# One more filler matmul at the end of each pair, at the head of the wide wo loop and in its steps

## The chip, the cores and the metric

The kernel runs on one core of one Trainium2 chip. The metric is the device time in microseconds (us). A time is the median of several runs, and differences of well under one per cent matter here only as far as they stand clear of the spread of the runs. TensorE is written PE, VectorE DVE, ScalarE ACT, SyncE (which issues the loads) SP.

## The reference

A gated mix of two branches for one token of width 512. Branch A is decode attention over 32 heads with a cache of 16384 positions; branch B is a small gated MLP. Cut to what matters:

```python
g = sigmoid((x * gate_w).sum(-1, keepdims=True))
q = (x @ wq)                       # 32 heads of 128
scores = q @ k_cache.T * 128**-0.5 # k_cache: (1, 32, 16384, 128) bf16
p = softmax(scores)
o = p @ v_cache                    # v_cache: the same shape
a = o.reshape(1, 1, 4096) @ wo     # wo: (4096, 512)
b = gmlp(x, w_in, w_sp, b_sp, w_out)
return g * a + (1 - g) * b
```

The two caches are 134 MB each. Every byte is used once.

## The kernel before

The heads are taken two at a time: 16 pairs. A pair has 8.39 MB of keys and 8.39 MB of values, loaded into three buffers in turn. DVE multiplies the keys by the query, PE sums the products with identity matmuls, ACT makes the exponentials, and PE multiplies them with the values. A load into a buffer is issued by SP when the buffer's last user has signalled.

`fill` is the helper the change uses. It issues 512-column matmuls into a scratch bank whose contents nobody reads. They do no work; they keep PE busy in gaps, so that its clock is not throttled. They load no weights of their own and write partitions 96 and up, so they sit in the last of the four column groups of the array. `warm` does the same over the full width, with weights.

```python
def warm(e, n):
    for j in range(n):
        args = (m_ps[0], ident[:, :], zero[:, :])
        ...  # the first loads the weights, the others repeat with the same ones

def fill(e, m, n=1):
    for _ in range(n):
        matmul_again(nc, e, m_ps[0][96:96 + m, :], ident[:, 0:m], zero[:, :], start=True,
                     stop=True, skip_group_check=True)
```

The end of a pair: a loop of value matmuls, then two fillers, then the wait for ACT's drain of the bank, then four small fp32 matmuls whose end releases the value buffer.

```python
def values(e, p, pa, va):
    ...
    with e.Fori(0, NT) as t:               # 8 steps
        ...                                # 8 value matmuls into d_ps
        ins.then_inc(pv_s, 1)              # ACT drains d_ps after the eighth
        fill(e, 8)
        ...
    o2 = o_ps[:, bass.ds(value(e, p, NP - 1) * 2, 2)]
    fill(e, 8, 2)
    take(e, drn_s)                         # waits for ACT
    for r in range(4):
        ins = e.matmul(o2, lhsT=d_sb[:, r * Dh:(r + 1) * Dh],
                       rhs=pick[:, r * 2:(r + 1) * 2], ...)
    ins.then_inc(pe.sem, 1)                # the value buffer is free
```

After the last pair comes the product with `wo`: four "wide" steps of four matmuls, one in each column group, then 32 narrow matmuls in the first two column groups, in order of the pieces in which `wo` is loaded.

```python
def pe_wide(e):
    ...
    warm(e, 3)
    with e.Fori(0, WIDE // WG) as t:       # 4 steps
        ...                                # 4 matmuls, one in each column group
        ins.then_inc(pe.sem, 1)
        fill(e, 1)
        ...
```

The one choice at the end of a pair is made here:

```python
with nc.body("pe_values", valid_engines=kind):
    values(e, p, pa, va)
    e.reg_alu(p, p, 1, ALU.add)
    e.br_lt(i, NP, on_true="pe_scores", on_false="pe_more")
```

The softmax here doesn't subtract the row's maximum and nothing guards it: scores larger than these inputs give would overflow.

## Time and profile before

| | before |
|---|---|
| median of 3 runs | 651.58 us (651.5 to 651.92) |
| loaded | 279.60 MB, 430 GB/s over the span |
| busy: PE, DVE, ACT | 65%, 52%, 7% |
| one pair's loads at 430 GB/s | 16.78 MB, 39.0 us |

The page of the kernel before: its span, the line of PE's busy time with its share of the span, the busy tenths of the loading engines in 40 equal slices, and what they moved.

```profile
span 650.2 us, 7779 instructions
...
PE 423.5 (65%) x2474; PEld 47.0 (7%) x1312; DVE 335.2 (52%) x156; ACT 46.1 (7%) x114; POOL 2.6 (0%) x11
...
DMA  9999989999999999999999999999999999999898
...
DMA packets 6203, 279.60 MB, mean 430 GB/s; under 512 B 695, under 2 KB 826, under 8 KB 1210
```

Every slice of the DMA row is at 8 or 9 tenths, while no computing engine is above two thirds. 279.60 MB divided by 650.2 us is the 430 GB/s: the whole span is loading.

The view of the line that issues the cache loads, kernel before; the times run from issue to landing.

```profile
DMA to landing us min/median/max: 24.6/34.7/55.0
```

A whole key or value load of 8.39 MB needs 19.5 us at 430 GB/s. Even the quickest load took 24.6 us, so an estimated 5 us (24.6 less 19.5) of older loads stood ahead of it.

The timeline of the kernel before at the end of a pair. Columns: start, duration, engine, line, operation, what it wrote and read, count, and in brackets the idle time before it and what ended that.

```profile
555.13 0.81 PE L91 MATMUL ps_all<-zero,ident 128*8 128x512 bf16 x3
...
556.13 0.59 ACT L606 CAST ps_all<-zero 128x512 f32<-128x512 bf16 x1
...
557.02 1.05 PE L531 MATMUL ps_all<-pick,d_sb 128*128 128x2 f32 x8 [1.08 <-PEq L86]
558.10 0.80 SPq L647 DMA_DIRECT2D bufs<-in_A_k_cache_dram  x2
```

The three fillers at 555.13 are the last one of the value loop and the two of the pair end. PE then sits idle for 1.08 us until ACT has drained and cleared the bank, and the matmuls with `pick` start at 557.02. SP issues the next key load as soon as they are done.

The tail of the kernel before, the same view.

```profile
638.46 0.60 PE L106 MATMUL ps_all<-bufs,p_t 128*8 x8
...
643.38 0.39 PE L106 MATMUL ps_all<-bufs,o 128*1 x4 [0.32 <-PEq L86]
...
645.69 0.39 PE L106 MATMUL ps_all<-bufs,o 128*1 x4 [0.19 <-PEq L86]
...
645.97 1.04 PE L724 MATMUL ps_all<-bufs,o 128*1 128x256 bf16 x16
...
647.28 0.42 PEld L724 LDWEIGHTS ps_all<-bufs,o 128*1 128x1 bf16 x10 [0.36 <-DMA bufs<-in_A_wo_dram]
...
647.96 0.09 PEld L724 LDWEIGHTS ps_all<-bufs,o 128*1 128x1 bf16 x4 [0.26 <-DMA bufs<-in_A_wo_dram]
648.23 0.08 PEld L724 LDWEIGHTS ps_all<-bufs,o 128*1 128x1 bf16 x2 [0.19 <-DMA bufs<-in_A_wo_dram]
...
648.58 0.41 DVE L739 CAST res<-ps_all 1x256 bf16<-1x256 f32 x1 [6.04 <-PE ps_all L724]
```

The last step of value matmuls starts at 638.46 and the final cast of the result at 648.58. The weight loads (PEld) at 647.28, 647.96 and 648.23 are each shown waiting for a piece of `wo`.

### The profile page before, as it was taken

How to read it: one execution, taken by the hardware profiler on the slowest of the kernel's cores; microseconds unless marked ns; L12 is line 12 of the kernel's file. 1: busy time of each engine (PE TensorE's matmuls, PEld its weight loads, DVE VectorE, ACT ScalarE, POOL GpSimd, SP SyncE). 2: the span in 40 equal slices, each digit the busy share in tenths (PEclk: the TensorE clock that was granted, in tenths of full speed). 3: DMA queues.
4: the chain of work that ended last, by engine and by line, in shares of the span. 5: the costliest groups of instructions: out<-in, count | busy, mean ns of one | idle time of the engine just before them, and what ended most of it. 6: DMA issues, size and time to landing. Idle time of an engine off the chain costs nothing. (4 is left out here: it accounts for less than half of the span.)

```text
span 650.2 us, 7779 instructions
## 1 busy us (share of the span) xinstructions
PE 423.5 (65%) x2474; PEld 47.0 (7%) x1312; DVE 335.2 (52%) x156; ACT 46.1 (7%) x114; POOL 2.6 (0%) x11
## 2 busy tenths in 40 slices
PE   0646687847477574857757486584748857478678
PEld 0000000000101000010000101000010100001022
DVE  3457839256280835618165370835628174465600
ACT  2220000100001000010100001000000100001011
POOL 1000000000000000000000000000000000000000
PEclk9959798958889796888969679796977969698979
DMA  9999989999999999999999999999999999999898
GB/s 384 463 419 452 452 387 452 452 444 395 452 452 395 444 452 444 395 452 452 407 431 452 444 395 452 452 427 411 452 452 391 448 452 439 399 431 472 390 431 342
DMA packets 6203, 279.60 MB, mean 430 GB/s; under 512 B 695, under 2 KB 826, under 8 KB 1210
## 3 DMA queue, kind: packets, MB, share of 16 engines
q1 hardware_dynamic: 6194, 279.58, 99.6%
q8 instruction: 1, 0.02, 0.0%
q10 hardware_dynamic: 8, 0.00, 0.0%
HBM read 279.58 MB, written 0.00 MB: 430 GB/s over the span
## 5 line engine op out<-in xcount | busy, mean ns | idle before, releaser
L579 DVE TENSOR_TENSOR bufs<-bufs,qb x64 | 281.4, 4418 | 171.8 <-DVEq L86 171.8
L91 PE MATMUL ps_all<-bufs,ident 128*128 x960 | 257.7, 422 | 0.0
L496 PE MATMUL ps_all<-bufs,ident 128*128 x64 | 28.8, 450 | 154.7 <-PEq L86 154.5
L106 PE MATMUL ps_all<-bufs,p_t 128*8 x1024 | 82.3, 395 | 30.3 <-PEq L86 20.3
L564 DVE TENSOR_REDUCE s_sb<-ps_all 128x64 f32<-128x512 f32 x64 | 44.0, 688 | 92.1 <-DVEq L86 92.1
L91 PE MATMUL ps_all<-zero,ident 128*8 128x512 bf16 (+2 forms) x167 | 59.4, 388 | 0.0
L592 ACT ACTIVATE p_t<-s_sb 64x256 f32 x32 | 13.3, 414 | 462.5 <-ACTq L86 462.1
L496 PEld LDWEIGHTS ps_all<-bufs,ident 128*128 128x128 bf16 x64 | 6.3, 99 | 365.3 <-issue 365.3
L106 PEld LDWEIGHTS ps_all<-bufs,p_t 128*8 x1024 | 19.3, 83 | 163.3 <-issue 161.9
L531 PE MATMUL ps_all<-pick,d_sb 128*128 128x2 f32 x128 | 17.3, 257 | 16.5 <-PEq L86 16.5
L531 PEld LDWEIGHTS ps_all<-pick,d_sb 128*128 128x128 f32 x128 | 16.0, 195 | 34.8 <-issue 34.8
L601 ACT COPY d_sb<-ps_all 128x512 f32<-128x512 f32 x16 | 9.4, 586 | 105.3 <-ACTq L86 105.3
L606 ACT CAST ps_all<-zero 128x512 f32<-128x512 bf16 x15 | 8.8, 589 | 1.7
L675 DVE RECIPROCAL rl<-ps_all 128x32 f32<-128x32 f32 x1 | 0.4, 358 | 12.3 <-PE ps_all L552 12.3
L381 DVE TENSOR_TENSOR bufs<-ps_all,ident 128x896 f32<-128x896 f32 x2 | 2.1, 1086 | 8.7 <-PE ps_all L91 8.7
L676 DVE SCALAR_TENSOR_TENSOR o_sb<-ps_all,g_sb,rl 128x32 bf16<-128x32 f32 x1 | 0.3, 251 | 11.7 <-PE ps_all L531 11.7
L592 ACT ACTIVATION_READ_ACCUMULATOR p_t<-s_sb x32 | 5.9, 185 | 0.0
L321 PE MATMUL ps_all<-xgw,const-float32-1.0 1*128 1x3 f32 x2 | 0.6, 359 | 8.0 <-DVE xgw L317 8.0
L91 PE MATMUL ps_all<-bufs,xb 128*128 x12 | 5.0, 547 | 0.0
L106 PE MATMUL ps_all<-bufs,u 128*1 x14 | 2.6, 372 | 3.1 <-ACT ps_all L427 2.4
L345 PE MATMUL ps_all<-bufs,xb 128*128 x4 | 2.3, 574 | 3.3 <-DMA bufs<-in_B_w_in_dram 3.3
L301 DVE MEMSET ps_all<- 128x3584 f32 x1 | 3.0, 3045 | 1.9 <-PEq L770 1.9
(76 smaller groups left out, 40.9 us busy)
## 6 DMA issues: line engine op xcount, KB each, us to landing
bufs<-in_A_k_cache_dram SPq DMA_DIRECT2D x2, 4096.0 KB, 36.3
bufs<-in_A_v_cache_dram SPq DMA_DIRECT2D x1, 5120.0 KB, 34.5
bufs<-in_A_wq_dram SPq DMA_DIRECT2D x1, 4096.0 KB, 12.4
bufs<-in_A_v_cache_dram SPq DMA_DIRECT2D x1, 2048.0 KB, 39.1
bufs<-in_A_wo_dram SPq DMA_DIRECT2D x1, 2048.0 KB, 25.5
bufs<-in_B_w_in_dram SPq DMA_DIRECT2D x1, 1792.0 KB, 15.6
bufs<-in_A_v_cache_dram SPq DMA_DIRECT2D x1, 1024.0 KB, 41.1
bufs<-in_A_wo_dram SPq DMA_DIRECT2D x1, 1024.0 KB, 27.7
```

Of the source, the lines that this page charges most:

```text
L91: ins = eng.matmul(out, lhsT=lhsT, rhs=rhs, **flags).ins
L106: ins = eng.matmul(bank[0:m, 0:n], lhsT=lhsT, rhs=rhs, **flags).ins
L301: dve.op(lambda e: e.memset(ps_all[:, 0:7 * 512], 0.0), mark=True)
L345: if n else matmul_on(nc, e, lambda: e.matmul(args[0], lhsT=args[1], rhs=args[2], **flags), [at, (xa, 0)]))
L381: dve.op(lambda e, h=h, zh=zh: e.tensor_tensor(out=zm[:, 2 * h * ZB:2 * (h + 1) * ZB].rearrange("p (b m k) -> p b m k", b=2, k=FhC), in0=z ...
L496: matmul_on(nc, e, lambda: e.matmul(s3, lhsT=ident[:, :], rhs=k3[:, :, 0:W], start=True, **flags), [(kw, 0)])
L531: ins = e.matmul(o2, lhsT=d_sb[:, r * Dh:(r + 1) * Dh], rhs=pick[:, r * 2:(r + 1) * 2], start=False, stop=False, skip_group_check=True)
L564: return e.tensor_reduce(out=s_sb[:, c * QK:(c + 1) * QK], in_=s_ps[c % 2].rearrange("p (j w) -> p j w", w=W), axis=AX.X, op=ALU.add)
L579: e.tensor_tensor(out=k3, in0=k3, in1=qi, op=ALU.mult).then_inc(mul_s, 1)
L592: e.activation(out=p_t[rows, bass.ds(at, NG * 8)].rearrange("p (t c) -> p t c", c=8)[:, :, 4 * s:4 * s + 4], in_=s_sb[rows, :].rearrange(" ...
L601: return e.copy(out=d_sb[:, :], in_=d_ps)
L606: e.copy(out=d_ps, in_=zero[:, :]).then_inc(drn_s, 1)
```

## The change

The likely intent is to keep PE warmer by filling a little more of its gaps: a third filler at the pair end, a fourth warming matmul ahead of the wide loop, and a second filler in each wide step. In all, 16 + 1 + 4 = 21 more instructions are executed on PE; no other engine's order changes.

```diff
@@ values @@
         o2 = o_ps[:, bass.ds(value(e, p, NP - 1) * 2, 2)]
-        fill(e, 8, 2)
+        fill(e, 8, 3)
         take(e, drn_s)
@@ pe_wide @@
-        warm(e, 3)
+        warm(e, 4)
         with e.Fori(0, WIDE // WG) as t:
@@ the same loop @@
             ins.then_inc(pe.sem, 1)
-            fill(e, 1)
+            fill(e, 1, 2)
```

## The prediction

> **What bounds the kernel now.** Loading. The page's header lines give 279.60 MB moved in a 650.2 us span, 430 GB/s mean, and 37 of 40 slices of the DMA row are at 9. The Trainium skill, "DMA: Bandwidth & Descriptors", section "Where 436 GB/s comes from", puts the fabric's ceiling at 435 GB/s; the trace's 430 agrees and the change does not touch it. PE is 65% busy, DVE 52%, ACT 7%.
>
> The cache loads stay queued. An 8192 KB load needs 19.5 us at 430 GB/s, but the loads' own line shows issue to landing at 24.6 us at the least, 34.7 median. So at least about 5 us of older work (estimate: 24.6 - 19.5) stood ahead of each, and a buffer freed a few tenths later starves nothing.
>
> **What the change adds.** Only PE instructions. A filler is a 512-column matmul into a scratch bank; back to back the trace starts them 0.21 us apart at full clock, about 0.43 us at half clock.
>
> 1. *Pair end, 16 times, one more filler.* In the timeline of the pair ending at 558 us, the fillers begin at 555.13 and end at 555.94. ACT drains and clears the bank until 556.72, and the fp32 matmuls with `pick` start at 557.02, released by that. PE idles 1.08 us; the filler fills 0.21 us of it. Delay: 0. In the last pair the gap is 0.37 us, still more than 0.21. The filler cannot keep the clock up: after a pair PE has nothing for up to 8 us, and the granted clock falls to 0.50 (stretches 522 to 530). The Trainium skill, "TensorE: Matmul & The Clock Gate", section "What's actually happening", speaks of about 3.4 us of idleness to go cold; 0.21 us does not close 8.
>
> 2. *Head of the wide wo loop, one more.* Three fillers run from 642.24; their streaming ends about 642.9. The first loop matmul starts at 643.38, released by a semaphore. The fourth fits.
>
> 3. *Its four steps, one more each.* A step takes 0.76 us from start to start, with PE's stream filled for about 0.43 us (0.21 matmuls, 0.21 filler). A second filler makes 0.64, still inside; I allow 0 to 0.03 us for its issue. After the last step the extra filler may hold the next matmul (645.97) by 0.15 to 0.2 us.
>
> **What of it reaches the end.** The clock is already 1.00 there (stretches from 638 us on), so nothing runs faster. The last pieces of wo hold the end: the weight loads at 647.28, 647.96 and 648.23 are each shown waiting for DMA (0.36, 0.26, 0.19 us). A lag of 0.2 us at 646 is mostly absorbed there; I carry 0 to 0.15 us.
>
> **Predicted time:** 651.6 us, range 651.0 to 652.3 (mostly the spread of runs, 651.5 to 651.92 before). Faster by over 2%: 0.005; within 2%: 0.99; slower by over 2%: 0.005.
>
> **What would show it.** Right: the pair-end gap of PE before the `pick` matmuls goes from 1.08 to about 0.87 us while their start stays; loop steps stay near 0.76 to 0.80 us; the last weight loads still wait for DMA; GB/s 430. Wrong: steps of 0.9 us or more; no DMA wait before the last wo matmuls.
>
> **What would make it wrong.** A last pair run at half clock, where the third filler would delay the tail by up to 0.4 us; or another chip with another loading rate.

## The result, and the profile after

| | before | after |
|---|---|---|
| median of 6 runs | 651.57 us (651.5 to 651.92) | 651.64 us (651.53 to 652.76) |
| ratio, 95% interval | | 1.0003 (0.999 to 1.0016) |
| last value step to final cast | 10.12 us | 10.15 us |
| mean granted clock, profiled run | 0.850 | 0.856 |

A ratio is the mean time of one kernel's fast runs over the mean of the other's in the same rounds, so it is not quite the ratio of the medians in the table.

The page after, the same lines:

```profile
span 650.1 us, 7801 instructions
...
PE 432.3 (66%) x2496; PEld 45.6 (7%) x1312; DVE 335.5 (52%) x156; ACT 46.1 (7%) x114; POOL 2.6 (0%) x11
...
DMA  9999999999999999999999999999999999999998
...
DMA packets 6203, 279.60 MB, mean 430 GB/s; under 512 B 695, under 2 KB 826, under 8 KB 1210
```

PE is busy 8.8 us longer (432.3 less 423.5), and the span and the loading are as before.

The line of the cache loads, after:

```profile
DMA to landing us min/median/max: 24.2/34.3/54.9
```

The end of a pair, after:

```profile
554.70 1.03 PE L91 MATMUL ps_all<-zero,ident 128*8 128x512 bf16 x4
...
555.70 0.59 ACT L606 CAST ps_all<-zero 128x512 f32<-128x512 bf16 x1
...
556.59 1.05 PE L531 MATMUL ps_all<-pick,d_sb 128*128 128x2 f32 x8 [0.86 <-PEq L86]
557.67 0.80 SPq L647 DMA_DIRECT2D bufs<-in_A_k_cache_dram  x2
```

There are four fillers now. The gap is 0.86 us in place of 1.08, shorter by the one filler. From the start of the last ACT instruction to the `pick` matmuls it is 0.89 us in both kernels (557.02 less 556.13; 556.59 less 555.70). The filler sits wholly inside time in which PE waited for ACT.

The tail, after:

```profile
638.35 0.61 PE L106 MATMUL ps_all<-bufs,p_t 128*8 x8 [0.16 <-PEq L86]
...
643.27 0.39 PE L106 MATMUL ps_all<-bufs,o 128*1 x4
...
645.58 0.39 PE L106 MATMUL ps_all<-bufs,o 128*1 x4
...
645.86 0.38 PE L724 MATMUL ps_all<-bufs,o 128*1 128x256 bf16 x4
...
646.02 0.38 PE L91 MATMUL ps_all<-zero,ident 128*1 128x512 bf16 x1
...
647.17 0.41 PEld L724 LDWEIGHTS ps_all<-bufs,o 128*1 128x1 bf16 x10 [0.35 <-DMA bufs<-in_A_wo_dram]
...
647.87 0.09 PEld L724 LDWEIGHTS ps_all<-bufs,o 128*1 128x1 bf16 x4 [0.28 <-DMA bufs<-in_A_wo_dram]
648.16 0.08 PEld L724 LDWEIGHTS ps_all<-bufs,o 128*1 128x1 bf16 x2 [0.20 <-DMA bufs<-in_A_wo_dram]
...
648.50 0.41 DVE L739 CAST res<-ps_all 1x256 bf16<-1x256 f32 x1 [6.07 <-PE ps_all L724]
```

The step from 643.27 to the last at 645.58 takes 2.31 us for three steps, as before (643.38 to 645.69). The next matmul follows the last step's start by 0.28 us in both. The waits for pieces of `wo` are still there (0.35, 0.28, 0.20 us). From the last value step (638.35) to the final cast (648.50) it is 10.15 us against 10.12.

### The profile page after: what moved, and what is told of

The parts are those of the page before. It is cut to its first block, busy times and chain, and to the rows that moved or that the text cites. A ratio compares the mean times of both kernels' runs of the same rounds, so it can differ in the third digit from the quotient of the medians.

```text
span 650.1 us, 7801 instructions
## 1 busy us (share of the span) xinstructions
PE 432.3 (66%) x2496; PEld 45.6 (7%) x1312; DVE 335.5 (52%) x156; ACT 46.1 (7%) x114; POOL 2.6 (0%) x11
## 5 line engine op out<-in xcount | busy, mean ns | idle before, releaser
L91 PE MATMUL ps_all<-bufs,ident 128*128 x960 | 264.3, 431 | 0.0
L496 PE MATMUL ps_all<-bufs,ident 128*128 x64 | 28.3, 442 | 151.3 <-PEq L86 151.3
L106 PE MATMUL ps_all<-bufs,p_t 128*8 x1024 | 80.1, 387 | 29.3 <-PEq L86 18.7
L91 PE MATMUL ps_all<-zero,ident 128*8 128x512 bf16 (+2 forms) x188 | 63.4, 384 | 0.0
## 6 DMA issues: line engine op xcount, KB each, us to landing
bufs<-in_A_v_cache_dram SPq DMA_DIRECT2D x1, 1024.0 KB, 39.8
```

The source lines that it names most:

```text
L91: ins = eng.matmul(out, lhsT=lhsT, rhs=rhs, **flags).ins
L106: ins = eng.matmul(bank[0:m, 0:n], lhsT=lhsT, rhs=rhs, **flags).ins
L496: matmul_on(nc, e, lambda: e.matmul(s3, lhsT=ident[:, :], rhs=k3[:, :, 0:W], start=True, **flags), [(kw, 0)])
```

## The experiments

All experiments start from the changed kernel, and each was timed against the kernel before in rounds on the same chip. Three theories were tested.

- A: the kernel is bound by loading. At the pair end there are two layers of slack: the gap in PE, and loads that are queued. In the tail the slack is a few tenths of a microsecond.
- B: the pair end is on the path, and one filler was free only because it fitted into the gap.
- C: the fillers pay for themselves by a warmer clock, and this offsets what they cost.

Three groups were run, each on one chip: the first with late12, late80, wide6 and keep36 (before: 651.68 us), the second with late40, none_end, none_all and bytes (before: 651.86), the third with mid40, none_wide, none_pair and keepmid (before: 651.63, 651.38 to 652.3).

| run | median us | ratio to before (95%) |
|---|---|---|
| bytes | 637.31 | 0.9777 (0.9761 to 0.9793) |
| late12 | 651.52 | 0.9996 (0.9979 to 1.0012) |
| late40 | 659.08 | 1.0103 (1.0085 to 1.0122) |
| mid40 | 652.70 | 1.0016 (0.9999 to 1.0032) |
| late80 | 768.60 | 1.1787 (1.1768 to 1.1807) |
| wide6 | 653.43 | 1.0025 (1.0008 to 1.0042) |
| none_end | 653.18 | 1.0017 (1.0000 to 1.0034) |
| none_all | 653.91 | 1.0037 (1.0019 to 1.0054) |
| none_wide | 652.83 | 1.0012 (0.9995 to 1.0028) |
| none_pair | 652.75 | 1.0020 (1.0004 to 1.0037) |
| keep36 | 652.80 | 1.0015 (0.9998 to 1.0032) |
| keepmid | 652.62 | 1.0015 (0.9998 to 1.0031) |

### bytes: is it the loading?

```diff
+        if kind == "v" and 3 <= i < NP - 1:
+            cuts = (0, KP - 16)      # the last sixteenth is not loaded
```

> A kernel that is wrong on purpose: twelve of the value loads (pairs 3 to 14) leave out their last sixteenth, 12 x 0.524 MB = 6.29 MB, and all arithmetic is as in the changed kernel (on stale values). Theory A (bound by loading): 6.29 MB at 430 GB/s is 14.6 us, so 637.0 us, from 635.5 to 639. Rival B (bound by TensorE's pair or the releases): within 1 us of 651.6.

Measured: 637.31 us, 14.55 us below before, where 14.6 was worked out from the bytes alone. The values used are stale; the arithmetic is that of the changed kernel. The page shows fewer bytes at the same rate:

```profile
DMA packets 6203, 273.31 MB, mean 430 GB/s; under 512 B 695, under 2 KB 826, under 8 KB 1210
```

Theory A's first half holds: time follows bytes.

### late12, late40, mid40, late80: how much slack has the pair end?

```diff
+        kind = [e.engine]
+        e.br_lt(p, NP - 1, on_true="pe_late", on_false="pe_close")   # mid40: NP - 3
+        with nc.body("pe_late", valid_engines=kind):
+            fill(e, 8, 12)                                           # 40, 40, 80
+            nc.br("pe_close", engines=kind)
+        nc.switch_bb("pe_close")
         o2 = o_ps[:, bass.ds(value(e, p, NP - 1) * 2, 2)]
         fill(e, 8, 3)
```

> Twelve further fillers at the end of every pair but the last, ahead of the wait for the drain. Twelve at 0.21 us are 2.6 us; 0.86 us of it fits in the gap, so the pick matmuls and the release of the value buffer come about 1.7 us later in 15 pairs. Theory A (the kernel is bound by loading, and a freed buffer's load is queued behind at least about 5 us of older loads): 651.6 us, within 0.5 us of the kernel before. Rival B (the pair end is on the path and the one filler was free only because it fitted in the gap): 15 x 1.7, so about +25 us. Rival C (fillers pay for themselves by a warmer clock): faster, by more than noise.

Measured: 651.52 us, no difference. Its timeline at the end of a pair:

```profile
555.66 3.62 PE L91 MATMUL ps_all<-zero,ident 128*8 128x512 bf16 x16
...
559.20 1.05 PE L537 MATMUL ps_all<-pick,d_sb 128*128 128x2 f32 x8
```

Sixteen fillers in a row took 3.62 us and the `pick` matmuls started without any gap, so the release did come late, in fifteen pairs, and cost nothing. Theory B, which asked for 25 us, is out. Theory C is out too for this place: PE was busy 463.5 us and its clock was 0.89 in the mean, and no time was won.

> Forty further fillers at the end of every pair but the last: 8.5 us, 7.7 us beyond the gap. TensorE's period per pair is then about 35 us, still below the 39 us of a pair's loads. Theory A (a release that is late is hidden while older loads are queued; the key loads, which the pick matmuls release, land 41.0 us after their issue in the median, 21 us more than their own 19.5 us): 651 to 655 us, GB/s 428 or more. Rival B2 (the smallest slack of any load, about 5 us, is what counts at every pair): 15 x 2.7, about +40 us.

Measured: 659.08 us, 7.2 us slower. That is above what A gave and far below B2's 40. The stretches show where it was not lost. First the changed kernel, then the run with forty (the same columns); the last column is GB/s, the one before it the DMA share, the third from the end PE's clock.

```profile
core 0: us, PE busy (x) PEld busy (x) DVE busy (x) ACT busy (x) POOL busy (x), PEclk, DMA share, GB/s
80.00:240.00 160.00, 109.93 (x629) 10.07 (x314) 86.74 (x37) 9.30 (x27) 0.00 (x0) 0.87 1.00 433
240.00:400.00 160.00, 108.16 (x643) 10.57 (x352) 80.22 (x32) 9.21 (x26) 0.00 (x0) 0.85 1.00 434
400.00:560.00 160.00, 103.77 (x608) 10.86 (x320) 80.12 (x32) 9.93 (x26) 0.00 (x0) 0.86 1.01 437
```

```profile
80.00:240.00 160.00, 139.45 (x807) 10.02 (x330) 87.58 (x37) 9.76 (x28) 0.00 (x0) 0.97 1.00 433
240.00:400.00 160.00, 136.75 (x803) 10.39 (x344) 80.13 (x32) 9.58 (x26) 0.00 (x0) 0.98 1.00 433
400.00:560.00 160.00, 136.56 (x774) 9.71 (x304) 80.13 (x32) 9.09 (x25) 0.00 (x0) 0.98 1.01 436
```

The loading rate is the same within 1 GB/s in all three stretches, 433, 433 and 436 against 433, 434 and 437. The tail shows where it was lost:

```profile
646.53 0.60 PE L106 MATMUL ps_all<-bufs,p_t 128*8 x8
...
656.12 0.41 DVE L745 CAST res<-ps_all 1x256 bf16<-1x256 f32 x1 [5.51 <-PE ps_all L730]
```

The last value step starts at 646.53, eight microseconds after the changed kernel's 638.35, and the rest follows it in about 9.6 us. Yet the last piece of the last value load was no later: issued at 605.2 us and 33.1 us to landing, so there at 638.3, against 638.1 in the changed kernel (598.3 and 39.8). So PE was late and not the loads: the fillers of the last pairs before the end ran when hardly any work was left to hide them, and pushed PE's last work past the end of the loads. My expectation had overlooked that this dose falls into the tail.

> The forty late fillers again, but only in the first 13 of the 16 pairs. In the run with forty in 15 pairs the loads ended at about 647.5 us as always and only the last pair came late, so its 7 us should have come from the fillers of pair 15 pushing the tail, not from the loads. Theory A: without them in the last three pairs the time is back at 651.6, within 0.6 us, though 13 pairs release their value buffer 7.7 us later. Rival B2 (each late release loses some loading time): +6 us remain, 657 to 658.

Measured: 652.70 us, 1.07 us above before, where 0.6 was allowed and B2 asked for 6. Thirteen releases that came 7.7 us late did not cost a loss each; B2 is out. (The run leaves the fillers out of the fourteenth and the fifteenth pair; it does not tell these two apart.) The remaining microsecond is before the tail:

```profile
639.25 0.60 PE L106 MATMUL ps_all<-bufs,p_t 128*8 x8 [0.77 <-PEq L86]
...
649.39 0.41 DVE L745 CAST res<-ps_all 1x256 bf16<-1x256 f32 x1 [6.06 <-PE ps_all L730]
```

From the last value step (639.25) to the final cast (649.39) it is 10.14 us, the same as in the changed kernel. The whole tail starts 0.9 us later, because the last piece of the last value load landed that much later, at 639.0 us (598.2 and 40.8) against 638.1. Whether the fillers cause that is not settled; see keepmid below.

> Eighty further fillers at the same place: 17 us, 16 us beyond the gap. TensorE's own period per pair is then about 26 us busy before plus 17 us, against the 39 us that a pair's 16.8 MB takes at 430 GB/s. Theory A says slack is finite, so this must cost: I expect +40 to +120 us, with the loads landing within about 20 us of their issue and the mean rate falling well below 430 GB/s. Rival B: 15 x 16, so +240 us. If the time stays at 652, even theory A's account of the slack is wrong (it would be much larger than I read).

Measured: 768.60 us, 117 us slower, at the top of the range. The page of that run: PE's busy time, and the mean loading rate.

```profile
PE 658.6 (86%) x3696; PEld 43.6 (6%) x1312; DVE 335.4 (44%) x156; ACT 46.0 (6%) x114; POOL 2.6 (0%) x11
...
DMA packets 6203, 279.60 MB, mean 364 GB/s; under 512 B 695, under 2 KB 826, under 8 KB 1210
```

Now the rate falls to 364 GB/s. The loads land 21.8 us after their issue in the median, in place of 34.3 in the changed kernel, where a load itself needs 19.5; the queue ahead of them is nearly gone. PE is busy 86% of the span, and the same kind of load is issued every 45.25 us in the timeline, against 39.0 us that a pair's bytes take. In one such cycle (342.73 to 387.98 us) PE waits only 4.35 us (2.21, 1.03 and 1.11). PE's own cycle, with these waits in it, has become the limit. So slack at the pair end exists, is finite, and is many times one filler.

### wide6: how much slack has the tail?

```diff
-            fill(e, 1, 2)
+            fill(e, 1, 6)
```

> Six fillers in each wide wo step in place of two. If the matmuls of the next group are held behind the fillers of their own column group (0.21 us for the last of the four value matmuls plus six at 0.21 us), a step takes about 1.5 us instead of 0.76, and the last step ends about 2.2 us later. Theory A (the tail has about 0.2 to 0.3 us of slack before the last wo loads): +1.9 us at the end if the following matmuls overtake the fillers that are in another column group, +2.9 us if they are held behind the last five fillers. Rival B (the tail has room for anything below the load, so fillers in it never show): within 0.3 us of before.

Measured: 653.43 us, 1.75 us slower. Its timeline:

```profile
647.81 0.38 PE L106 MATMUL ps_all<-bufs,o 128*1 x1
647.82 0.38 PE L724 MATMUL ps_all<-bufs,o 128*1 128x256 bf16 x4
...
649.11 0.38 PE L91 MATMUL ps_all<-zero,ident 128*1 128x512 bf16 x1
...
650.40 0.41 DVE L739 CAST res<-ps_all 1x256 bf16<-1x256 f32 x1 [7.97 <-PE ps_all L724]
```

The last wide matmul starts at 647.81, 2.23 us after the changed kernel's last step at 645.58, and the final cast comes at 650.40, 1.90 us later than there. So the tail absorbs 0.33 us, and the rest is paid. That is the first of A's two numbers (+1.9), and theory B's "the tail has room for anything" is out.

The order of the records is worth a look. The fillers of the last step come before the narrow matmuls in the program. Yet a narrow matmul (L724) starts at 647.82 and the sixth of those fillers at 649.11. So matmuls bound for other column groups went past fillers that stand before them in the program. In the changed kernel the same shows in small: L724 at 645.86, the second filler at 646.02.

### none_end, none_all, none_wide, none_pair: what do the fillers do at all?

```diff
@@ values @@                       # none_end, none_all, none_pair
-        fill(e, 8, 3)
@@ pe_wide @@                      # none_end, none_all, none_wide
-        warm(e, 4)
+        warm(e, 1)
@@ pe_wide, the loop @@            # none_end, none_all, none_wide
-            fill(e, 1, 2)
@@ values, the loop @@             # none_all only
-            fill(e, 8)
```

> All the fillers that the change touches taken out: none at the pair end, one warming matmul ahead of the wide loop in place of four, none in its steps. Theory A: the body is unchanged (the granted clock in the gaps was at half speed already), so only the tail can lose, by the last 36 wo matmuls at half clock at the most, 0 to 1.7 us: 651.5 to 653.3 us. Rival C (the fillers buy time in every pair): tens of us slower, as each pair's matmuls would run cold.

> As the last one, and the one filler in each step of the value loop taken out too. Theory A: TensorE's busy time and clock may fall anywhere in the body and the loads stay at 430 GB/s; only the tail can lose, in which the last pair's value loop may run at half clock: 651.5 to 655 us. Rival C: slower by more than 1%.

> One half of the run without fillers: one warming matmul in place of four and none in the wide steps, the three at the pair end kept. If the clock in the tail is held by the fillers of the wide loop, the granted clock falls to 0.5 in it, the last wo matmuls take 0.21 us a couple in place of 0.11, and the time is 652.8 to 653.5, as without all of them (653.18). If the pair-end fillers hold it, 651.6, within 0.3 us.

> The other half: no filler at the pair end, four warming matmuls and two fillers in each wide step kept. Theory A: the pair end is off the path and the wide fillers hold the clock in the tail: 651.6, within 0.3 us. If the pair-end fillers are what keeps the tail warm, 652.5 to 653.5.

Measured: 653.18, 653.91, 652.83 and 652.75 us, so 1.1 to 2.1 us above before (for none_wide the 95% interval of the ratio includes 1). The loading did not slow: in none_all, PE's busy time fell to 398.5 us, the mean rate was 428 GB/s over the longer span, and the last piece of the last value load landed at 638.2 us, against 638.1 in the changed kernel. But not all of the loss is the clock's. In the profiled runs of none_wide and none_end the last value step began at 639.29 and 639.12, 0.94 and 0.77 us later than in the changed kernel, because the last piece of the last value load landed late, as in mid40; that is nearly half of what these two profiled runs lost. The rest lies after that step. The stretches of none_wide show what happens in its tail:

```profile
core 0: us, PE busy (x) PEld busy (x) DVE busy (x) ACT busy (x) POOL busy (x), PEclk, DMA share, GB/s
...
645.00:645.50 0.50, 0.36 (x4) 0.06 (x4) 0.00 (x0) 0.00 (x0) 0.00 (x0) 1.00 1.11 461
645.50:646.00 0.50, 0.27 (x4) 0.12 (x4) 0.00 (x0) 0.00 (x0) 0.00 (x0) 0.77 0.89 365
646.00:646.50 0.50, 0.32 (x4) 0.01 (x1) 0.00 (x0) 0.00 (x0) 0.00 (x0) 0.50 1.03 408
```

The clock falls from 1.00 to 0.50 at about 645.8 us. The same view of the changed kernel has 1.00 in every one of these stretches. The tail from the last value step to the final cast is then 11.14 us in none_wide (639.29 to 650.43), 11.25 in none_end (639.12 to 650.37) and 12.60 in none_all (638.38 to 650.98), against 10.15 in the changed kernel. So the fillers that the kernel already had are worth about 1.0 to 2.5 us of tail between them. In this run the loss of the wide ones let the clock fall in the tail; one of the four runs of none_wide was at 651.8 us all the same.

The clean split that I had expected between the wide and the pair-end ones did not come. none_pair too was slower, with two runs at 651.9 and two at 653.6 us, and its profiled run (651.93 us) shows the clock at 0.50 from about 642 to 644 and a tail of 10.70 us. Both kinds hold the clock, and how much one of them matters alone seems to vary from run to run; four runs are too few to say how much.

### keep36, keepmid: does a warm clock in the body pay?

```diff
-            e.br_lt(i, NP, on_true="pe_scores", on_false="pe_more")
+            e.br_lt(i, NP, on_true="pe_keep", on_false="pe_more")   # keepmid: only while i < NP - 2
+        with nc.body("pe_keep", valid_engines=kind):
+            warm(e, 36)
+            nc.br("pe_scores", engines=kind)
```

> Thirty-six fillers (7.7 us at full clock) after the pick matmuls and after the release of the value buffer, before the next scores, so that TensorE does not go cold in the gap of up to 8 us. The mean granted clock should rise from 0.86 to 0.93 or more, and the score matmuls should come to about 380 ns each from 431. Theory A: the time stays at 651.6, within 0.5 us, because TensorE bounds nothing there. Rival C (a warm clock is what the fillers are for, and pays): faster by several us (60 us of busy PE time is saved at most, a part of it on the path).

> The thirty-six fillers that keep TensorE warm between pairs, but not ahead of the scores of the last two pairs, so that the wo loads are issued as early as in the changed kernel. The run with them in all pairs was 1.1 us slower, its bulk of loads ended as always at about 647.5 us, and one last wo piece landed 1.1 us after it. If that came of the late issue of the wo loads, this one is at 651.6, within 0.4 us, with the clock at 0.93 or more. If it came of the extra work in the body, 652.7 again. Rival C (a warm clock in the body pays): below 651.

Measured: 652.80 and 652.62 us, with mean clocks of 0.971 and 0.958. The clock was kept up in nearly the whole body, the score matmuls took 388 ns in keep36 in place of 431 (380 foreseen), and the time did not fall: theory C is out. It even rose by about 1 us, which A did not foresee; the 95% intervals of both runs still include no change. In the profiled run of keep36 one piece of `wo` landed late, and the weight load of the last two matmuls waited 1.27 us for it:

```profile
649.28 0.08 PEld L727 LDWEIGHTS ps_all<-bufs,o 128*1 128x1 bf16 x2 [1.27 <-DMA bufs<-in_A_wo_dram]
```

In that of keepmid the last value step came at 639.32, and from there the tail took the usual 10.13 us. So in both the microsecond is a last piece of a load landing late, though not the same piece. The late issue of `wo` that I had blamed for it is not the cause, since keepmid has it without. It is not shown that the added PE work is the cause either: none_wide, whose edit lies wholly after that point, had its last value step at 639.29 in the same group, and single runs of the kernel before reached 652.3 to 652.93 in the three groups. The landing times of the last value piece fall into two sets. Eight profiled runs have it at 638.1 to 638.3 us: before, after, late12, late40, wide6, keep36, none_all and none_pair. Four have it at 639.0 to 639.1: mid40, keepmid, none_wide and none_end. late40 has more fillers than mid40 and is among the early ones, so the added PE work does not sort them. What does stays open, with one profiled run of each.

## Why the prediction was right

- *Bound by loading*: right. bytes moved the time by 14.55 us for 6.29 MB.
- *The pair end has slack*: right in both layers. The gap went from 1.08 to 0.86 us (0.87 foreseen) and in the last pair from 0.37 to 0.15; releasing the buffer 1.7 us late (late12) or 7.7 us late (mid40, apart from the open microsecond) did not cost time.
- *The filler cannot keep the clock up between pairs*: right (0.50 from 522 to 530 us in the changed kernel too), and it would not have mattered. keep36 kept it up with 36 and won nothing.
- *The fourth warming matmul fits*: right. The loop began 1.03 us after the cast of `o2` started, against 1.04 before (643.27 less 642.24; 643.38 less 642.34).
- *Steps stay*: right, 2.31 us for three steps in both.
- *The extra filler may hold the next matmul by 0.15 to 0.2 us*: this term of the sum was mis-sized. It measured 0: the next matmul follows 0.28 us after the last step's start in both kernels. It goes to other column groups and did not wait for the filler. I had worked with strict program order.
- *The last pieces of wo hold the end, and absorb a lag*: half of it. Slack is there, 0.33 us by wide6, but PE's own chain from the last value piece is the other limit, only that much behind. In mid40 and keepmid the end moved with the last value piece and PE hardly waited for `wo`.
- *Nothing runs faster because the clock is 1.00 in the tail already*: right for the profiled runs. Taking fillers away shows that the old ones are needed for it; the extra ones had nothing left to hold up.

The expected sum was 0 to 0.15 us. The medians differ by 0.07 us, which is inside the spread of the runs, so the number alone does not test the terms; the traces do. There was some luck in it: two of the six runs of the changed kernel took 652.02 and 652.76 us, perhaps with the late landing, and the stated range ends at 652.3.

## What to carry to other kernels

A filler is free where its engine waits anyway, so look at what ends the gap and compare the filler's time with the gap, not with the span. To know whether the slack behind it is real, overdose it: twelve fillers cost nothing, eighty cost 117 us, and a dose that reaches into the last stage is paid almost whole (1.90 of 2.23 us in wide6) whatever the body has to spare. A clock that is already at full in the only stage that computes on the path has nothing more to give.

## What the Trainium skill lacked or had wrong

- "TensorE: Matmul & The Clock Gate", section "Step-by-step: what each phase is for", says that matmuls stay in program order and that only weight loads are pulled ahead. The records here show otherwise across column groups: in wide6 a narrow matmul starts at 647.82 us, and a filler that stands before it in the program starts at 649.11; in the changed kernel it is 645.86 against 646.02. "TensorEngine Tiling (Array Packing)", section "Key Properties", does say that tiles operate independently, but not that this changes the order of starts.
- "TensorE: Matmul & The Clock Gate", section "What's actually happening", ties the fall to half clock to an idle window of about 3.4 us. The section "A second HAM failure mode: psum-queue depth-cycling" of the same page does name frequent short idles as a cause, and the trace fits that better: in none_wide the clock fell at about 645.8 us although PE had no gap longer than 0.75 us after 643.5; from 643.5 to 645.5 it was busy 0.77 us of 2.0 (0.00 + 0.29 + 0.12 + 0.36). How busy is busy enough is on no page, and these runs do not settle it either.
- "DMA: Bandwidth & Descriptors", section "Where 436 GB/s comes from", says that for transfers between HBM and SBUF the HBM side binds at about 358 GB/s. Taken alone the sentence misleads: with one core running, this kernel holds 430 GB/s over 650 us, near the fabric's 435. The note in the section "Measured" above it puts the 358 right, as a core's share when both cores of an HBM domain stream.
- No page tells how much the landing of one load varies. The last piece of the last value load landed at 638.1 to 638.3 us in eight profiled runs and at 639.0 to 639.1 in four (keep36, keepmid above), a step of about 0.8 us, half as wide as the whole spread of the kernel before (651.38 to 652.93 us).
